# Two product columns and half an output block moved ahead of a score block, in a gated linear attention with a bilinear feed-forward on one core

## The chip, the cores and the metric

The kernel runs on one core of a Trainium2 chip, as one launch. The metric is the device time of a run in microseconds; the time of a kernel is the median over its runs. The engines are named as in the profile: PE is TensorE's matrix multiplication and PEld its weight load, DVE is VectorE, ACT is ScalarE, POOL is GpSimd and SP is SyncE. PSUM is the memory that PE writes its results to; the kernel uses it as eight banks, 0 to 7. SBUF is the core's working memory.

## The reference

For 4 batches with 8 heads of 48 numbers and 768 steps, a state of 48 x 48 per head decays by `alpha`, takes in `k` times `v`, and is read by `q`. The result, 3072 tokens by 384, goes through a bilinear feed-forward of width 1536.

```python
for t in range(S):
    state = alpha[:, :, t, :, None] * state + np.einsum('bhd,bhe->bhde', k[:, :, t], v[:, :, t])
    y[:, :, t] = np.einsum('bhd,bhde->bhe', q[:, :, t], state)
...
x = attn_out.transpose(0, 2, 1, 3).reshape(B * S, H * D)
a = x @ w_a
b = x @ w_b
out = a * b @ w_out
```

## The kernel before

The steps are cut into six chunks, numbered 0 to 5; each holds 256 steps of two of the four batches, and its two batches are called u = 0 and u = 1. A chunk goes through two parts. The recurrence part takes logarithms of `alpha`, sums them along the steps by matrix multiplications, scales `q` and `k` with the exponentials, and computes scores between steps, masks them, multiplies them with `v`, adds what the carried state gives, and updates the state. The feed-forward part computes twelve columns `a` and twelve columns `b` of 128 numbers each, multiplies them element by element, and multiplies the products with `w_out`, in four output blocks of 128 tokens.

The order of all of this is written out by hand in a text, `PROGRAM`. Each line is `chunk: step; step; ...`, and the program is emitted exactly in that order. Every engine runs its own steps in the order of the text, one after the other, and waits at a step until what the step reads has been written and what it overwrites has been read. So a step's place in the text sets its place in the queue of each engine that it uses. A digit behind a matrix step is the PSUM bank that it writes (scores `D` and out tiles `SB` take that bank and the next).

The steps that matter here, with the line of the profile on which their instructions appear:

- `a f w i`, `b f w i` (L784): product column f for one half w of a chunk's tokens, or for all of them (`*`): three matmuls on PE into bank i. The half takes 256 columns of tokens.
- `as f w` (L790): ACT copies column `a` from PSUM to SBUF. `pr f w` (L798): DVE multiplies that copy with column `b`, which it reads from PSUM, into `prod`.
- `o m h i` (L806): half h of output block m, six matmuls on PE. The first half opens bank i, the second one (`-`) adds to it. `ot m E` (L821 on ACT, L823 on DVE) brings the block to SBUF, `st m Y` stores it from SP's queue.
- `D u h i` (L672): scores of batch u, four heads, 16 matmuls on PE. `Mc` (L681) copies them on ACT to the tile `m`, `Mm` (L685) masks that tile on DVE; `M` (L677) does both on DVE.
- `SB u i` and `SA u` (L701): 16 matmuls each, the part that the carried state gives. `Y u` (L722): 32 matmuls with the masked scores. `X u E` (L762) brings the result to SBUF, and `XT u` (L769) turns it by a DMA on SP's queue into `xT`, which the product columns read.
- `k u g E` (L660 and L661): two instructions on DVE that update the state.
- `ln` (L418): the logarithms, one long instruction on ACT. `R 0`, `R 1` (L495, tiles `lh` and `ll`): rests of the pair sums on DVE. `AQ i` (L505): the sums along the steps on PE, into banks i and i + 1. `lv` (L524): scaling of `q` or `k`, here on POOL.

The place of the change is lines 129 to 141 of the kernel. There the feed-forward of chunk 1 is worked in between the last scores of chunk 2 and the sums of chunk 3:

```
2: SB 1 3; D 0 1 1; Mc 0 1; Mm 0 1 V; k * 1 V
3: R 1
1: o 2 1 -; ot 2 S
0: st 2 Y
1: st 2 Y
2: D 0 0 5; Mc 0 0; Mm 0 0 V; SB 0 1; SA 1; Y 1; X 1 S; XT 1
1: a 4 1 7
4: ln *
1: as 4 1; b 9 1 0; pr 9 1; o 0 0 5
3: AQ 3
2: SA 0; Y 0; X 0 S; XT 0
5: ld a * Y
1: o 0 1 -; ot 0 V; a 1 1 6; a 10 1 1; as 1 1; as 10 1
```

`SB 1 3` opened banks 3 and 4 for batch 1, `SB 0 1` opens banks 1 and 2 for batch 0. `AQ 3` uses banks 3 and 4 again, and `a 10 1 1` uses bank 1 again.

Of the kernel before, what the change touches and what calls it, by code (L numbers as in the profile page):

```python
# [130 lines left out]
1: o 2 1 -; ot 2 S  # L131
0: st 2 Y
1: st 2 Y
2: D 0 0 5; Mc 0 0; Mm 0 0 V; SB 0 1; SA 1; Y 1; X 1 S; XT 1
1: a 4 1 7
4: ln *
1: as 4 1; b 9 1 0; pr 9 1; o 0 0 5
3: AQ 3
2: SA 0; Y 0; X 0 S; XT 0
5: ld a * Y  # L140
1: o 0 1 -; ot 0 V; a 1 1 6; a 10 1 1; as 1 1; as 10 1
3: E 0 b; E 0 i
1: b 4 1 2; pr 4 1; b 8 1 5; b 1 1 1; a 8 1 6; b 10 1 0; pr 1 1; o 3 0 2; pr 10 1; as 8 1; pr 8 1; o 3 1 -; ot 3 S; st 3 Y
2: a 4 * 7; as 4 *
# [818 lines left out]
```

## Time and profile before

| | |
|---|---|
| time, median of 3 runs | 194.72 us (194.59 to 195.71) |
| the profiled execution | 195.32 us, of which its span is 193.5 us |
| granted clock of TensorE over the span | 1.00 |
| ACT, DVE, POOL busy | 103.3 us, 138.4 us, 50.8 us |

The span is the stretch from the first to the last instruction that the profile shows; all places below are microseconds from its start. The timeline has one row for each run of like instructions: start, length, engine, line, operation, what it writes and reads, and behind an x how many. A note in brackets says how long the engine was idle before it and who ended that. The chain of waits goes from the end of the program back, at each step to what released it. "issue" in it is time in which the engine waited for nothing that the profile shows. Ends of matmuls are modelled, so a row of matmuls may reach into the next one.

### The profile page before, as it was taken

The numbers are of one execution on the slowest core, as the hardware profiler recorded it, in microseconds if no ns is written. First come the engines' busy times: TensorE is split into PE (matmuls) and PEld (weight loads), VectorE is DVE, ScalarE is ACT, GpSimd is POOL, SyncE is SP. The second block draws the span as 40 slices with busy tenths as digits, with TensorE's granted clock in tenths as the row PEclk, the third lists the DMA queues.
The fourth block names the chain that finished last, engine by engine and source line by source line (L and its number), as shares of the span: only waits on it lengthen the run. The fifth ranks groups of instructions, "written<-read, shape, count | busy, mean of one in ns | idle before, by whom it ended". The sixth has DMA issues, their size and how long they took to land.

```text
span 193.5 us, 5877 instructions
## 1 busy us (share of the span) xinstructions
PE 184.7 (95%) x2509; PEld 111.4 (58%) x2509; DVE 138.4 (71%) x230; ACT 103.3 (53%) x189; POOL 50.8 (26%) x71
## 2 busy tenths in 40 slices
PE   7889699999999998999999999999999999999993
PEld 3467475666687865744556644555544566544462
DVE  4688777999899799597979499875854871156520
ACT  4565575886775676556565235875255622154401
POOL 8999645850640425000400020050000000000000
PEclk9999999999999999999999999999999999999999
DMA  5999999999999999489995488999297005021013
GB/s 139 261 214 211 243 247 251 252 246 260 243 220 231 198 234 219 57 233 213 172 219 69 100 203 178 118 191 120 59 180 160 3 3 122 0 99 67 0 42 122
DMA packets 67162, 30.96 MB, mean 160 GB/s; under 512 B 58064, under 2 KB 65120, under 8 KB 67136
## 3 DMA queue, kind: packets, MB, share of 16 engines
q0 software_dynamic: 18640, 14.16, 41.3%
q1 hardware_dynamic: 48352, 16.34, 39.9%
q8 instruction: 19, 0.31, 0.7%
q10 hardware_dynamic: 144, 0.10, 0.2%
q14 instruction: 7, 0.06, 0.1%
HBM read 25.98 MB, written 4.74 MB: 159 GB/s over the span
## 4 chain that ended last, share of the span: by engine, by line
PE 84%; POOL 6%; DMA 5%; issue 2%; DVE 1%; ACT 0%; POOLq 0%; DVEq 0%
PE psum L784 47%; PE psum L806 24%; DMA wb_t<-in_moe_w_b_dram 5%; PE psum L672 3%; PE psum L722 2%; PE psum L625 2%; PE psum L696 2%; PE psum L701 1%; PE psum L505 1%; PE psum L817 1%; POOL v_t L411 1%; POOL a_t L411 1%; PE psum L591 1%; POOL wa_t L391 1%; DVE prod L798 1%
## 5 line engine op out<-in xcount | busy, mean ns | idle before, releaser
L784 PE MATMUL psum<-xT,wb_t 128*128 128x512 bf16 (+1 forms) x270 | 57.0, 337 | 1.3 <-DMA wb_t<-in_moe_w_b_dram 1.3
L784 PE MATMUL psum<-xT,wa_t 128*128 128x512 bf16 (+1 forms) x270 | 56.1, 337 | 0.0
L806 PE MATMUL psum<-wo_t,prod 128*128 128x384 bf16 x276 | 48.5, 326 | 0.0
L784 PEld LDWEIGHTS <-wb_t 128*128 128x128 bf16 x270 | 25.5, 98 | 21.9 <-DMA wb_t<-in_moe_w_b_dram 1.6
L784 PEld LDWEIGHTS <-wa_t 128*128 128x128 bf16 x270 | 25.6, 98 | 19.7 <-issue 0.2
L806 PEld LDWEIGHTS <-prod 128*128 128x128 bf16 x276 | 26.1, 98 | 17.0
L681 ACT ACTIVATE m<-psum 128x1024 bf16<-128x1024 f32 x16 | 16.3, 1023 | 6.1 <-PE psum L672 5.9
L823 DVE COPY ot<-psum 128x384 f32<-128x384 f32 (+1 forms) x13 | 6.9, 538 | 15.7 <-PE psum L806 13.2
L524 POOL TENSOR_TENSOR q_t<-q_t,ra 128x384 f32<-128x384 f32 x8 | 8.8, 1103 | 34.7 <-DVE prod L798 18.4
L821 ACT ACTIVATE ot<-psum 128x384 f32<-128x384 f32 (+1 forms) x12 | 5.7, 477 | 12.9 <-PE psum L806 11.9
L524 POOL TENSOR_TENSOR k_t<-k_t,a_t 128x384 f32<-128x384 f32 x5 | 6.0, 1197 | 22.8 <-DVE QKp L550 17.9
L685 DVE TENSOR_TENSOR m<-m,mask 128x1024 bf16<-128x1024 bf16 x16 | 11.6, 734 | 0.3 <-ACT m L681 0.2
L418 ACT ACTIVATE la<-a_t 128x1536 f32<-128x1536 f32 (+2 forms) x9 | 9.5, 1053 | 3.7 <-DMA a_t<-in_alpha_dram 3.7
L550 DVE TENSOR_TENSOR QKp<-k_t,invb 128x768 bf16<-128x768 f32 x10 | 11.0, 1105 | 0.2
L677 DVE TENSOR_TENSOR m<-psum,mask 128x1024 bf16<-128x1024 f32 x8 | 9.8, 1219 | 1.6 <-PE psum L672 1.5
L550 DVE TENSOR_TENSOR QKp<-q_t,beta 128x768 bf16<-128x768 f32 x10 | 9.3, 947 | 0.0
L672 PE MATMUL psum<-kqT 64*64 64x128 bf16 x384 | 8.6, 218 | 0.2 <-DVE kqT L599 0.2
L411 POOL DMA_DIRECT2D v_t<-in_v_dram x8 | 8.6, 1075 | 0.6 <-PE psum L784 0.5
L762 ACT ACTIVATE ys<-psum 128x768 bf16<-128x768 f32 x7 | 5.6, 808 | 5.6 <-PE psum L722 3.3
L672 PEld LDWEIGHTS <-kqT 64*64 64x64 bf16 x384 | 6.3, 107 | 2.7 <-issue 2.3
L411 POOL DMA_DIRECT2D a_t<-in_alpha_dram x6 | 6.3, 1043 | 5.6 <-DVE prod L798 2.9
L444 PE MATMUL psum<-wz 128*128 128x512 bf16 x17 | 5.5, 473 | 1.2 <-DVE og L336 1.2
(272 smaller groups left out, 272.0 us busy)
## 6 DMA issues: line engine op xcount, KB each, us to landing
out_dram<-ot SPq DMA_DIRECT2D x23, 192.0 KB, 2.6
a_t<-in_alpha_dram POOLq DMA_DIRECT2D x3, 768.0 KB, 14.2
k_t<-in_k_dram SPq DMA_DIRECT2D x3, 768.0 KB, 6.7
q_t<-in_q_dram POOLq DMA_DIRECT2D x2, 768.0 KB, 12.8
v_t<-in_v_dram POOLq DMA_DIRECT2D x4, 384.0 KB, 9.2
q_t<-in_q_dram SPq DMA_DIRECT2D x2, 768.0 KB, 6.7
a_t<-in_alpha_dram POOLq DMA_DIRECT2D x3, 384.0 KB, 5.7
q_t<-in_q_dram POOLq DMA_DIRECT2D x3, 384.0 KB, 13.1
```

The costliest lines, as they stand in the source:

```text
L411: eng.dma_start(out=t[:, us, hs].rearrange("p b h r d -> p (b h) (r d)"), in_=src[ch.b0 + us.start:ch.b0 + us.stop, hs, ch.s * 2 * C:(ch.s ...
L418: nc.scalar.activation(out=ch.la[:, us, hs].rearrange("p b h r d -> p (b h r d)"), in_=ch.a[:, us, hs].rearrange("p b h r d -> p (b h r d) ...
L524: eng.tensor_mul(x, x, by)
L550: eng.tensor_mul(QKp[ch.c % 2][:, u, j, :, hs, :D], src[:, u, hs].rearrange("p h r d -> p r h d"), f)
L672: nc.tensor.matmul(s2[g * HC:(g + 1) * HC, r, p, rk, :], lhsT=ch.kqT[u][rs, 1, rk, 2 * h + p, g * HC:(g + 1) * HC], rhs=queriesT(ch, u, 2 ...
L677: nc.vector.tensor_mul(m.rearrange("p r a k s -> p (r a) (k s)"), ch.s2[u, h].rearrange("p r a k s -> p (r a) (k s)"), maskn(4))
L681: nc.scalar.activation(out=m.rearrange("p r a k s -> p (r a) (k s)"), in_=ch.s2[u, h].rearrange("p r a k s -> p (r a) (k s)"), func=AF.Copy)
L685: eng.tensor_mul(x, x, maskn(4))
L784: nc.tensor.matmul(p, lhsT=(wa_t, wb_t)[w][:, kk, f * 128:(f + 1) * 128], rhs=ch.xT[:, us.start // 2:us.stop // 2, kk].rearrange("p u g s ...
L806: nc.tensor.matmul(op, lhsT=ch.prod[:, f, at:at + C], rhs=wo_t[:, f, :], start=(f == 0), stop=(f == NFF - 1))
L821: nc.scalar.activation(out=o_, in_=i_, func=AF.Copy)
L823: eng.tensor_copy(o_, i_)
```

## The change

The product columns `a 4 1` and `b 9 1`, the copy and the multiplication that belong to them (`as 4 1`, `pr 9 1`), and the first half of output block 0 go ahead of the scores `D 0 0` of chunk 2. Their banks become 5, 6 and 7 in place of 7, 0 and 5. The second half of output block 0, with its copy to SBUF, goes from behind `Y 0` to behind `Y 1`. No step is added or taken away.

```diff
@@ -131,14 +131,14 @@
 1: o 2 1 -; ot 2 S
 0: st 2 Y
 1: st 2 Y
+1: a 4 1 5; as 4 1; b 9 1 6; pr 9 1; o 0 0 7
 2: D 0 0 5; Mc 0 0; Mm 0 0 V; SB 0 1; SA 1; Y 1; X 1 S; XT 1
-1: a 4 1 7
+1: o 0 1 -; ot 0 V
 4: ln *
-1: as 4 1; b 9 1 0; pr 9 1; o 0 0 5
 3: AQ 3
 2: SA 0; Y 0; X 0 S; XT 0
 5: ld a * Y
-1: o 0 1 -; ot 0 V; a 1 1 6; a 10 1 1; as 1 1; as 10 1
+1: a 1 1 6; a 10 1 1; as 1 1; as 10 1
 3: E 0 b; E 0 i
```

## The prediction

> **What bounds the kernel now.** I read the page first, then the chain of waits around the change, then the timeline of each engine there.
>
> ```profile
> span 193.5 us, 5877 instructions
> PE 184.7 (95%) x2509; PEld 111.4 (58%) x2509; DVE 138.4 (71%) x230; ACT 103.3 (53%) x189; POOL 50.8 (26%) x71
> ...
> q8 instruction: 19, 0.31, 0.7%
> ```
>
> PE is busy for 95% of the span, so a time moves only where PE's idle time moves: the change adds and drops no instruction. The chain of waits from 70 us on shows where PE's idle time lies here (start, length, what):
>
> ```profile
> 70.69 1.08 PE psum L806 x6
> 71.77 0.35 PE psum L672 x16
> 72.11 0.12 PE psum L701 x16
> 72.23 1.26 issue
> 73.50 0.31 PE psum L701 x16
> 73.81 0.51 PE psum L722 x32
> 74.32 0.76 PE psum L784 x6
> 75.08 0.97 PE psum L806 x6
> 76.05 0.63 PE psum L505 x8
> 76.69 0.12 PE psum L701 x14
> 76.80 0.51 PE psum L722 x32
> ```
>
> Matched with the program of order: 70.69 is `o 2 1`, 71.77 the scores `D 0 0 5`, 72.11 `SB 0 1`, 73.50 `SA 1`, 73.81 `Y 1`, 74.32 `a 4 1 7` and `b 9 1 0`, 75.08 `o 0 0 5`, 76.05 `AQ 3`, 76.69 `SA 0`, 76.80 `Y 0`; `o 0 1`, `a 1 1` and `a 10 1` follow. There is one hole, 1.26 us ahead of `SA 1`, and the profile finds nothing that `SA 1` waited for. Behind it the chain is PE work piece by piece, with no second hole. So the change can gain 1.26 us at most here, and any new wait of PE costs its full length.
>
> What is the hole? Within 70.5 to 71.6 us the queue list shows one packet of the queue of kind "instruction" (packets, MB, share):
>
> ```profile
> q8 instruction: 1, 0.02, 6.6%
> ```
>
> Nineteen such packets carry 0.31 MB, 16 KB each, and PE has 2509 + 2509 instructions, about 19 times 256. I read the hole as PE's next instructions arriving late. That packet was under way before 71.70, where the first moved matmul will start, so the change shouldn't shift its arrival: the hole ends near 73.50 whatever PE does meanwhile. The Trainium skill ("Runtime: NRT & Kernel Launch", section "Instruction fetch mechanics") says that instructions are refilled in blocks of 16 KiB, 256 instructions, and that crossing a block is mostly hidden. The size agrees with the row; "hidden" would make the hole something else, which is a rival below.
>
> **The change part by part.** It moves `a 4 1`, `b 9 1` and `o 0 0` (12 matmuls) ahead of `D 0 0`, and `o 0 1` to just behind `Y 1`; with them `as 4 1` (ACT) goes ahead of `Mc 0 0`, `pr 9 1` (DVE) ahead of `Mm 0 0`, and `ot 0` (DVE) to behind `Mm 0 0` as before. It issues no DMA and changes nothing on POOL. On SP no entry passes another. The new banks are 5 and 6 for the two products. `D 0 0 5` writes banks 5 and 6, so it must now wait until `as 4 1` and `pr 9 1` have read them; before, both products used banks (7 and 0) that `D 0 0` doesn't touch. `pr 9 1` stands in DVE's queue behind everything written above it, `R 1` (L495, `ll`) last. DVE's timeline of before:
>
> ```profile
> 70.01 0.95 DVE L495 TENSOR_TENSOR lh<-l 128x768 f32<-128x768 f32 x1
> ...
> 71.79 0.69 DVE L685 TENSOR_TENSOR m<-m,mask 128x1024 bf16<-128x1024 bf16 x1 [0.24 <-ACT m L681]
> 72.40 0.55 DVE L660 TENSOR_TENSOR tmp<-psum,Sm 128x384 f32<-128x384 f32 x1
> 72.99 0.56 DVE L661 TENSOR_TENSOR S<-tmp,bl 128x384 bf16<-128x384 f32 x1
> 73.46 1.76 DVE L495 TENSOR_TENSOR ll<-lh 128x768 f32<-128x768 f32 x1
> 75.14 1.49 DVE L685 TENSOR_TENSOR m<-m,mask 128x1024 bf16<-128x1024 bf16 x1
> 76.56 0.44 DVE L798 TENSOR_TENSOR prod<-as__1484,psum 128x256 bf16<-128x256 bf16 x1
> ```
>
> DVE is full from 71.79 (`Mm 0 1`) over `k * 1` to the end of `R 1`. `Mm 0 0` starts at 75.14; that place is now `pr 9 1`'s, which ends at 75.14 + 0.44 = 75.58. Nothing ahead of it on DVE is touched, so this is when `D 0 0` may start. The starts on PE, for step lengths:
>
> ```profile
> 71.70 0.42 PE L672 MATMUL psum<-kqT 64*64 64x128 bf16 x16
> 73.74 0.57 PE L722 MATMUL psum<-v_t,m 64*128 64x48 bf16 x32
> 74.25 0.50 PE L784 MATMUL psum<-xT,wa_t 128*128 128x256 bf16 x3
> 74.59 0.49 PE L784 MATMUL psum<-xT,wb_t 128*128 128x256 bf16 x3
> 75.98 0.36 PE L505 MATMUL psum<-l,utb 64*64 64x384 bf16 x4
> 76.74 0.57 PE L722 MATMUL psum<-v_t,m 64*128 64x48 bf16 x32
> 77.24 1.15 PE L806 MATMUL psum<-wo_t,prod 128*128 128x384 bf16 x6
> 78.23 0.82 PE L784 MATMUL psum<-xT,wa_t 128*128 128x256 bf16 x6
> ```
>
> From start to start one product takes 0.33 (74.25 to 74.59), half an output block 0.99 (77.24 to 78.23), `Y` 0.5 (73.74 to 74.25, 76.74 to 77.24), `AQ` with `SA` 0.76 (75.98 to 76.74). The 78.23 row holds `a 1 1` and `a 10 1`. New PE order: `a 4 1` at 71.70, `b 9 1` 72.03, `o 0 0` 72.37, ready for `D 0 0` at 73.36. It starts at 75.6. First new wait: 2.2 us. With `D`, `SB`, `SA` at 0.35 + 0.12 + 0.12 = 0.59 from the chain (the 0.31 of the `SA` behind the hole is a restart), `Y 1` starts at 76.2, `o 0 1` at 76.7, and PE is ready for `AQ` at 77.7.
>
> Now ACT, whose rows are:
>
> ```profile
> 71.80 0.49 ACT L821 ACTIVATE ot<-psum 128x384 f32<-128x384 f32 x1
> 72.19 1.02 ACT L681 ACTIVATE m<-psum 128x1024 bf16<-128x1024 f32 x1
> 74.36 0.81 ACT L762 ACTIVATE ys<-psum 128x768 bf16<-128x768 f32 x1 [1.15 <-PE psum L722]
> 75.07 1.48 ACT L418 ACTIVATE la<-a_t 128x1536 f32<-128x1536 f32 x1
> ```
>
> `o 0 0 7` writes the bank that `ot 2` reads until 71.80 + 0.49 = 72.29: just free at 72.37, so nothing. `as 4 1` runs at once behind it, before 72.7: nothing. `Mc 0 0` (the 1.02 row) starts when `D 0 0` is through, 75.6 + 0.42 = 76.0, and ends at 77.1; `X 1` (0.81) follows at once and ends at 77.9. `AQ 3` writes the banks that `X 1` reads: it starts at 77.9, a second wait of 0.2, where 1.6 us of products and `o 0 0` used to cover `X 1`. Then `Y 0` at 78.66; its second half needs `Mm 0 0`, which DVE, idle since 75.58, does at 77.1 to 77.8 in its 0.69 of the 71.79 row: covered. `a 1 1` starts at 79.16. But `ln *` (1.48) stands between `X 1` and `X 0` on ACT. Before, it ran from 75.07 under PE's products; now it runs from 77.9 to 79.3, so `X 0` runs 79.3 to 80.1. `a 10 1 1` writes bank 1, which `X 0` reads, and `o 0 1`, which used to stand there for 0.99 us, is gone: `a 10` starts at 80.15, a third wait of about 0.65. Before, `a 10` started one product into the row of 78.23, at 78.56.
>
> Sum: 2.2 + 0.2 + 0.65 = 3.05 of new idle time, less the hole's 1.26 and its restart's 0.2: **+1.6 us**, the same as 80.15 - 78.56. Behind it the order is unchanged and PE works without a break, so nothing gives it back. The tightest neighbour is `XT 0`, a transpose by DMA which SP starts when `X 0` is through and whose result `a 4 *` needs:
>
> ```profile
> DMA to landing us min/median/max: 3.1/3.1/3.1
> 82.50 0.81 PE L784 MATMUL psum<-xT,wa_t 128*128 128x512 bf16 x3
> ```
>
> It would start at 80.15 and land at 83.3; PE comes at 82.50 + 1.6 = 84.1. Covered, with 0.8 to spare.
>
> Bounds. What I know least is `R 1`: the same operation took 0.95 at 70.01 and 1.76 at 73.46, where POOL was at work:
>
> ```profile
> 73.24 2.84 POOL L524 TENSOR_TENSOR k_t<-k_t,a_t 128x384 f32<-128x384 f32 x2 [4.47 <-DMA k_t<-in_k_dram]
> ```
>
> I take 1.76, since neither POOL's start (a DMA's landing) nor `R 1`'s moves; at 0.95 all of the sum from 75.6 on is 0.8 earlier, +0.8. `pr 9 1` could be stretched in the same way, by up to the 0.8 that `R 1` and `Mm 0 0` (1.49 against 0.69) show; it reads PSUM, so I take 0.44. The Trainium skill ("SBUF — State Buffer", section "SBUF: two separate sides") says that GpSimd and a VectorE operation with two SBUF inputs exclude each other for a whole instruction; the rows agree for `R 1`, and by it `pr 9 1` with one SBUF input is spared. Lastly, PE's next 256 instructions: their packet would be asked for up to 2 us later than before, so a second late arrival of up to about 0.4 beside the third wait is possible; I take 0.
>
> The profiled execution took 195.32, 1.8 over its span and 0.6 over the median, so its 196.9 becomes **194.72 + 1.6 = 196.3** for the median.
>
> **The rivals.** *The hole isn't there to be absorbed* (chance 0.18): the profiled execution is 0.6 slower than the median, and if ordinary ones have little or none of the hole, or it has another cause and stays ahead of `SA 1`, the new waits cost up to 1.6 + 1.26 = 2.9, 197.6. For it: the skill's "mostly hidden", and 195.71 as the highest of three runs; against it: the packet's place. *A free `R 1`* (0.13): if `k_t` lands only after `R 1` has begun, or much earlier, POOL and `R 1` don't meet, and it ends at 74.4: +0.8, 195.5. *The moved work fills the hole and costs nothing* (0.09): 12 matmuls of 1.66 us cover 1.26, `D 0 0` follows at once, 194.72 - 1.26 = 193.5. It decides on `pr 9 1`: it must start before about 73.0, ahead of `R 1`. DVE's rows speak against it, `k * 1` and `R 1` standing back to back from 72.40 to 75.2.
>
> **How the numbers follow.** The forecast has 0.60, with its own range 195.9 to 196.9 (0.4 less, 0.6 more). From 195.3 to 197.7 lie it, the free `R 1` and most of the first rival. One per cent, about what a measurement of this kernel can tell from no change, is 1.95 us: slower means above 196.67. Of the forecast some 0.17 lies there, with the first rival's 0.18: 0.35. Faster by over 1% needs more than the hole: 0.03 of the third rival. The rest, 0.62, is within 1%, on the slow side.
>
> **What would show it.** In the changed profile: the hole ahead of `SA 1` gone; `D 0 0` (L672) starting at about 75.6, 2.2 us after the end of `o 0 0`, released by DVE L798, with `ll` at 73.46 just ahead of that L798; L505 released by ACT L762; `la` (L418) at about 77.9 and an L784 at about 80.1 released by ACT L762. The prediction is wrong if L672 starts before 74.5, if a hole for no reason stays at `SA 1`, or if PE makes up time behind 80 us.

## The result, and the profile after

| | before | changed |
|---|---|---|
| median of 19 runs each | 195.06 us | 196.34 us |
| lowest and highest | 194.19, 196.05 | 195.51, 199.09 |
| profiled execution, span | 195.32, 193.5 | 196.22, 194.4 |

The ratio of the changed kernel to the one before is 1.0076, with a 95% interval of 1.0049 to 1.0102: slower by 1.5 us, where +1.6 was forecast; the two medians differ by 1.3 us. The ratios in this document are formed over the runs, not from the two medians, and leave out each run that lies over 1.5% above the fastest of its kernel, here the four from 198.49 to 199.09; with them the mean is 1.9 us over that of before. Ten of the changed kernel's 19 runs lie between 195.51 and 196.34, the other nine between 197.16 and 199.09; the runs of the kernel before have no such second group.

PE's waits between 66 and 86 us in the profile after (who waited for whom: us in total, times, longest), and PE's timeline from 72 us on, of which the small matmuls of L701 are left out:

```profile
PE psum L672 <- DVE prod L798: 1.2, 1, 1.2
PE psum L784 <- ACT ys L762: 0.5, 1, 0.5
```

```profile
72.48 1.14 PE L806 MATMUL psum<-wo_t,prod 128*128 128x384 bf16 x6
73.54 0.24 PE L672 MATMUL psum<-kqT 64*64 64x128 bf16 x1
74.95 0.41 PE L672 MATMUL psum<-kqT 64*64 64x128 bf16 x15 [1.17 <-DVE prod L798]
75.55 0.57 PE L722 MATMUL psum<-v_t,m 64*128 64x48 bf16 x32
76.05 1.15 PE L806 MATMUL psum<-wo_t,prod 128*128 128x384 bf16 x6
77.19 0.36 PE L505 MATMUL psum<-l,utb 64*64 64x384 bf16 x4
...
78.44 0.50 PE L784 MATMUL psum<-xT,wa_t 128*128 128x256 bf16 x3
79.42 0.49 PE L784 MATMUL psum<-xT,wa_t 128*128 128x256 bf16 x3 [0.47 <-ACT ys L762]
```

The hole ahead of `SA 1` is gone, and two new waits stand in its place. `D 0 0` issues one matmul, into bank 5, at 73.54, and then waits at the second, into bank 6, until `pr 9 1` (L798) has read it. `a 10 1` waits for `X 0` (L762). The releasers on DVE, ACT and POOL:

```profile
73.60 0.95 DVE L495 TENSOR_TENSOR ll<-lh 128x768 f32<-128x768 f32 x1
74.47 0.43 DVE L798 TENSOR_TENSOR prod<-as__1484,psum 128x256 bf16<-128x256 bf16 x1
```

```profile
75.41 1.02 ACT L681 ACTIVATE m<-psum 128x1024 bf16<-128x1024 f32 x1 [2.71 <-PE psum L672]
76.33 0.80 ACT L762 ACTIVATE ys<-psum 128x768 bf16<-128x768 f32 x1
77.02 1.49 ACT L418 ACTIVATE la<-a_t 128x1536 f32<-128x1536 f32 x1
78.55 0.81 ACT L762 ACTIVATE ys<-psum 128x768 bf16<-128x768 f32 x1
```

```profile
73.85 2.52 POOL L524 TENSOR_TENSOR k_t<-k_t,a_t 128x384 f32<-128x384 f32 x2 [4.93 <-DMA k_t<-in_k_dram]
```

`pr 9 1` stands directly behind `R 1`, as forecast, but `R 1` took 0.95 here, not 1.76: POOL began at 73.85, after `R 1` at 73.60; in the profile of before POOL was first (73.24 against 73.46). So this execution shows the smaller of the two losses. By starts, `a 10` runs at 79.42; PE ran 0.13 later already at `o 2 1` (70.75 against 70.62 in the PE timelines), so the stretch lost 79.42 - 78.56 - 0.13 = 0.73.

### The profile page after: what moved, and what is told of

Read it like the earlier page. It is cut to its first block, busy times and chain, and to the rows that moved or that the text cites. A ratio compares the mean times of both kernels' runs of the same rounds, so it can differ in the third digit from the quotient of the medians.

```text
span 194.4 us, 5876 instructions
## 1 busy us (share of the span) xinstructions
PE 186.0 (96%) x2509; PEld 112.6 (58%) x2509; DVE 136.3 (70%) x230; ACT 103.3 (53%) x189; POOL 50.6 (26%) x71
## 4 chain that ended last, share of the span: by engine, by line
PE 83%; POOL 6%; DMA 5%; DVE 2%; issue 1%; ACT 1%; POOLq 0%
PE psum L784 47%; PE psum L806 23%; DMA wb_t<-in_moe_w_b_dram 5%; PE psum L672 3%; PE psum L722 2%; PE psum L625 2%; PE psum L696 2%; PE psum L701 1%; PE psum L505 1%; PE psum L817 1%; POOL v_t L411 1%; POOL a_t L411 1%; DVE prod L798 1%; PE psum L591 1%; POOL wa_t L391 1%
## 5 line engine op out<-in xcount | busy, mean ns | idle before, releaser
L685 DVE TENSOR_TENSOR m<-m,mask 128x1024 bf16<-128x1024 bf16 x16 | 10.8, 686 | 1.8 <-ACT m L681 1.8
L672 PE MATMUL psum<-kqT 64*64 64x128 bf16 x384 | 8.8, 218 | 1.5 <-DVE prod L798 1.4
L672 PEld LDWEIGHTS <-kqT 64*64 64x64 bf16 x384 | 6.4, 107 | 4.2 <-issue 3.8
L762 ACT ACTIVATE ys<-psum 128x768 bf16<-128x768 f32 x7 | 5.5, 807 | 4.0 <-PE psum L701 2.3
```

The lines of the kernel that those rows point to most:

```text
L672: nc.tensor.matmul(s2[g * HC:(g + 1) * HC, r, p, rk, :], lhsT=ch.kqT[u][rs, 1, rk, 2 * h + p, g * HC:(g + 1) * HC], rhs=queriesT(ch, u, 2 ...
L685: eng.tensor_mul(x, x, maskn(4))
```

## The experiments

Each is timed in its own session against the kernel before, whose median there was 195.2 to 195.4; so ratios are compared, not times. Where a kernel has a line less (the first part alone, and those with early stores), the line numbers of its profile are one lower: L671 there is L672 here.

**The bank of `b 9 1`.** In the changed kernel, so that `D 0 0` no longer meets `pr 9 1`:

```diff
-1: a 4 1 5; as 4 1; b 9 1 6; pr 9 1; o 0 0 7
+1: a 4 1 5; as 4 1; o 0 0 7; b 9 1 0; pr 9 1
```

> The changed kernel with one difference: b 9 1 goes to bank 0, as before the change, and stands behind o 0 0 (bank 0 is free by then), so that the scores D 0 0 no longer wait for pr 9 1. Theory (most of the loss is D 0 0 waiting for pr 9 1): D 0 0 (L672) starts at about 73.8 with no wait for DVE, a 10 1 at 78.3 to 78.6, as in the kernel before (78.56); time 194.6 to 195.2, ratio to before 0.998 to 1.001. Rival (the loss comes from a 10 1 waiting for X 0, whose cover o 0 1 is gone, and from X 0's place on ACT): the wait for X 0 stays at 0.5 or more and the time at 195.8 or above, ratio 1.004 or more.

Measured: 195.73, ratio 1.0021 (0.9986 to 1.0056): most of the loss is gone. `D 0 0` starts at 73.60 and doesn't wait (`o 0 0` ahead of it waits 0.25 for `ot 2`). But nothing is gained either, and the chain of waits shows why:

```profile
73.67 0.35 PE psum L672 x16
74.02 0.25 PE psum L701 x32
74.27 0.51 PE psum L722 x32
...
77.18 0.33 PE psum L784 x2
77.50 1.92 issue
79.42 2.26 PE psum L784 x19
```

PE gets through `SA 1` without a hole and is ready for the third matmul of `a 1 1` at 77.5; there it waits 1.92 us for nothing that the profile shows. From `SA 1`'s first matmul to that one the kernel before has 16 + 32 + 3 + 3 + 6 + 12 + 16 + 32 + 6 + 2 = 128 matmuls, with a weight load each: 256 instructions, one instruction packet. What PE won at the one packet it lost at the next. Nor did `a 10` have to wait for `X 0`, which ended under the new hole. The place of the loss was as the theory had it. The time was not: 195.73 lies over its 194.6 to 195.2, and `a 10` comes behind 79.4 in place of 78.3 to 78.6.

**`pr 9 1` ahead of `R 1`.** In the changed kernel, DVE's order alone:

```diff
-3: R 1
 1: o 2 1 -; ot 2 S
...
 1: a 4 1 5; as 4 1; b 9 1 6; pr 9 1; o 0 0 7
+3: R 1
```

> The changed kernel with R 1 (chunk 3) moved behind pr 9 1 in the text; only DVE's order changes, the banks stay. Theory (pr 9 1 is late because it is queued behind R 1, 0.95 to 1.76 us): pr 9 1 starts at about 73.6 and D 0 0 at about 74.0 in place of 74.9 to 75.6; a 10 1 at about 78.5; time 194.7 to 195.3, and the spread of the runs smaller than the changed kernel's (195.5 to 199.1), because R 1's meeting with POOL no longer reaches PE. Rival (D 0 0 waits for something else, such as as 4 1 on ACT): D 0 0 stays at 74.9 or later and the time at 196.3.

Measured: 195.45, ratio 1.0000 (0.9971 to 1.0030). Of its 12 runs, eleven lie between 194.63 and 196.24; the twelfth, the profiled one, took 374.52 and isn't read. So this rests on the times alone: the expected start of `D 0 0` is seen in no trace of this kernel, but with the same order and the early stores, below, the wait is 0.3. The interval lies wholly under the changed kernel's. With the banks as changed, the place behind `R 1` in DVE's queue is what costs.

**Is the hole a late instruction packet?** In the kernel before, 12 small matmuls of zeros early on, where PE waits anyway:

```diff
-0: b 0 0 4; a 0 0 2; as 0 0; pr 0 0
+0: warm 12 4; b 0 0 4; a 0 0 2; as 0 0; pr 0 0
```

> The kernel before with 12 small matmuls of zeros (128 x 128) ahead of b 0 0 of chunk 0, where PE waits for a weight load anyway; everything behind them stands 24 PE instructions later in the instruction stream. Theory (the 1.26 us hole ahead of SA 1 is the next 256 PE instructions arriving late): the hole moves 12 matmuls earlier, to behind the 4th matmul of SB 0 1, with the same order of length, and the 17th to 20th wait nowhere. Rival (SA 1 waits for data or for a resource of its own): the hole stays ahead of SA 1, behind 16 matmuls of SB 0 1.

Measured: one execution, 197.24, which is not compared. In it the hole is not at the packet that begins in `SB 0 1` but at the following one, 128 matmuls on. PE's timeline of `Y 0`, which in the kernel before is one row of 32:

```profile
76.13 0.37 PE L722 MATMUL psum<-v_t,m 64*128 64x48 bf16 x16
77.12 0.32 PE L722 MATMUL psum<-v_t,m 64*128 64x48 bf16 x12 [0.63 <-DVE m L685]
78.85 0.22 PE L722 MATMUL psum<-v_t,m 64*128 64x48 bf16 x4 [1.41 <-issue]
```

The hole stands behind the 28th matmul of `Y 0`. The third of `a 1 1` less 12 is exactly that: two of `a 1 1`, six of `o 0 1`, four of `Y 0`. The step expected within `SB 0 1` was off by one packet; the rival, a need of `SA 1`'s own, is out. The packets' own times in the traces say the same: in each of the seven profiles of these experiments and of before that have such a hole, PE goes on 1.3 to 1.65 us after a packet of the instruction queue has ended (71.86 and 73.50 in the kernel before, 77.99 and 79.42 in `x_bank`, 77.41 and 78.85 here). A hole that is always at the same instruction number, whatever the instruction there does, whose neighbours wait for nothing, and that ends at about the same distance behind such a packet, is an instruction packet that comes late.

**The second part alone.** In the kernel before, `o 0 1` and `ot 0` go from behind `Y 0` to behind `o 0 0`.

> The kernel before with the second part of the change alone: o 0 1 and ot 0 go from behind Y 0 to behind o 0 0, ahead of AQ 3; the banks and everything else stay. Theory (o 0 1 was the cover of X 0): AQ 3 and Y 0 come 1.0 us later, a 10 1 waits 0.4 to 0.6 us for X 0 behind a 1 1, and the time is 0.4 to 0.6 over the kernel before, 195.4 to 195.7. Rival (X 0 is covered anyway): no wait, the time of before.

Measured: 195.69, ratio 1.0009 (0.9978 to 1.0040), too near to tell. Its chain of waits:

```profile
72.03 0.25 PE psum L701 x32
...
77.08 0.45 issue
```

The second row is a hole at the third matmul of `a 1 1`, right ahead of where `X 0` would be waited for. The first is `SB 0 1` and `SA 1` without a hole, though PE's program up to there is that of the kernel before: the packet began at 68.98 in this execution, not at 70.70. So the hole ahead of `SA 1` comes and goes with the packet's time. The experiment was repeated with the early stores below.

**POOL held back behind `R 1`.** In the changed kernel, a one-element copy on POOL that reads `R 1`'s tile goes ahead of the two scalings of `k`:

```diff
-3: ra 1; lv 1 q P; ld v * P; lv 0 k P; lv 1 k P
+3: ra 1; lv 1 q P; ld v * P
...
-3: R 1
+3: R 1; gater; lv 0 k P; lv 1 k P
```

> The changed kernel, with POOL's two scalings of k for chunk 3 held back until R 1 has written its tile (a one-element copy on POOL that reads R 1's tile stands ahead of them), so that POOL and R 1 never meet. Theory (R 1 takes 0.95 alone and up to 1.76 beside POOL, and D 0 0 waits for it through pr 9 1): R 1 0.95 in the profile, D 0 0 0.9 to 1.2 us behind o 0 0, time 195.9 to 196.2, at the low end of the changed kernel's runs (195.5 to 199.1) and without the runs above 197. Rival (the long runs of the changed kernel have another cause): the same spread as the changed kernel's, with nearly half of the runs above 197.

Measured: 196.18 (195.50 to 196.86), ratio 1.0047 (1.0026 to 1.0067). All ten runs lie under 197. DVE's timeline in its profile has `R 1` and `pr 9 1`:

```profile
73.83 0.95 DVE L495 TENSOR_TENSOR ll<-lh 128x768 f32<-128x768 f32 x1
74.70 0.43 DVE L798 TENSOR_TENSOR prod<-as__1482,psum 128x256 bf16<-128x256 bf16 x1
```

So the changed kernel's upper group of runs goes back to the meeting of POOL and `R 1`. The changed kernel itself was not run in that session; but with the early stores, below, its POOL begins at 74.52, when `R 1` is through, and none of its seven runs is over 196.55. The same edit of the kernel before:

> The kernel before with POOL's scalings of k for chunk 3 held back behind R 1, as was done to the changed kernel. Theory (in the kernel before no matmul waits for R 1 or for pr 9 1 in this stretch, so R 1's length does not reach PE): the time of before within 0.3, its spread unchanged. Rival (R 1's meeting with POOL costs the kernel before as well): faster by 0.4 or more.

Measured: 195.16, ratio 0.9994 (0.9966 to 1.0021): nothing. Before the change no matmul hung on `R 1` here; the change is what tied PE to it. That holds where the hole stands: in `b_shift`, without a hole at `SA 1` and with an `R 1` of 1.75, `Y 0` waits 0.63 for `Mm 0 0` behind it.

**A meeting made on purpose.** As above, and POOL's `lv 1 q` is put beside `k * 1`.

> The same, but POOL's scaling of q for batch 1 of chunk 3, which was done at 66 us, is put where DVE does k * 1 and R 1 (released by Mm 0 1); the scalings of k stay held back behind R 1. Theory: DVE is held up by POOL by 0.5 to 0.9 us ahead of pr 9 1, D 0 0 starts that much later than in x_gate, and the time is 0.5 to 0.9 over x_gate's, 196.6 to 197.0, or more where PE's longer idle time costs clock. Rival (DVE's delay doesn't reach PE): the time of x_gate.

Measured: 200.12, ratio 1.0151 (1.0088 to 1.0215), and no test of the theory. Without `lv 1 q` ahead of it, POOL's load of `v` was issued at 63.51 in place of 67.72, and the scores ahead of this stretch waited 4.3 us for their transpose by DMA; that the one brought the other is likely and not shown. `k * 1`'s second instruction did take 1.12 in place of 0.56 beside POOL. The case came about by itself in the next kernel.

**The first part alone.** In the changed kernel, `o 0 1` and `ot 0` go back behind `Y 0`.

> The first part of the change alone: the changed kernel with o 0 1 and ot 0 put back behind Y 0. Theory: D 0 0 waits for pr 9 1 as in the changed kernel (1.2 us, or 2 where R 1 meets POOL); AQ 3 then waits 0.9 to 1.1 us for X 1, which has lost the products that stood between; a 10 1 waits for nothing; 0.2 to 0.5 over the changed kernel, 196.5 to 196.9. Rival (moving o 0 1 is what costs): under 196.0.

Measured: 198.75, ratio 1.0139 (1.0090 to 1.0187), far over the 0.2 to 0.5 that were expected. PE's waits in its profile, the rows of DVE and POOL in the timeline, the chain, and the busy times by stretch (length, busy time and instructions of PE, PEld, DVE, ACT and POOL, granted clock, DMA share, GB/s):

```profile
PE psum L671 <- DVE prod L797: 2.0, 1, 2.0
PE psum L504 <- ACT ys L761: 1.1, 1, 1.1
```

```profile
73.54 1.75 DVE L494 TENSOR_TENSOR ll<-lh 128x768 f32<-128x768 f32 x1
```

```profile
73.49 2.66 POOL L523 TENSOR_TENSOR k_t<-k_t,a_t 128x384 f32<-128x384 f32 x2 [4.64 <-DMA k_t<-in_k_dram]
```

```profile
78.82 0.23 PE psum L700 x11
79.06 0.75 PE psum L721 x32
79.81 2.01 PE psum L805 x6
```

```profile
75.00:78.00 3.00, 1.23 (x83) 1.19 (x86) 1.34 (x3) 1.84 (x3) 1.15 (x1) 1.00 0.29 64
78.00:81.00 3.00, 3.00 (x65) 2.08 (x64) 0.00 (x0) 2.06 (x2) 0.00 (x0) 0.54 0.37 71
81.00:84.00 3.00, 3.00 (x25) 2.38 (x23) 1.40 (x3) 1.61 (x5) 0.00 (x0) 0.89 0.42 80
```

Both waits are as expected, the first in its long form: `R 1` met POOL and took 1.75. What was not expected stands behind them. The granted clock is 0.54 and 0.89 of full speed in two stretches of 3 us, so PE lost (0.46 + 0.11) x 3 = 1.7 us, and the six matmuls of `o 0 1` took 2.01, where the kernel before has 1.08. The Trainium skill ("TensorE: Matmul & The Clock Gate", section "Part 1: The HAM clock gate (the "warmup" mystery)") gives half rate after an idle window of about 3.4 us; here it fell after waits of 2.0 and 1.1 us with work between them; the measurement decides.

**Calmer transfers when the packet is asked for.** In the kernel before, two stores go into SP's queue where their blocks are ready:

```diff
-0: st 3 Y; o 1 1 -; ot 1 V
+0: st 3 Y; o 1 1 -; ot 1 V; st 0 Y; st 1 Y
...
-0: st 0 Y; o 2 1 -
+0: o 2 1 -
...
-0: st 1 Y
```

> The kernel before with the stores of output blocks 0 and 1 of chunk 0 put into SP's queue 9 us earlier, at 57 to 59 us behind the store of block 3, where they were ready; in the kernel before they go out from 67 us on, when PE's instruction packet is asked for. Theory (the packet is held up by other transfers): the packet starts earlier than 3.1 us behind the start of PE's block, the holes in PE at 72 to 79 us become shorter by 0.3 to 1.2 us in sum, and the time is 0.2 to 0.8 less than before, 194.3 to 195.1. Rival (the packet takes its 5 to 6 us whatever else moves): the time of before.

Measured: 194.81, ratio 0.9974 (0.9952 to 0.9996), faster than either kernel, if only just clear of the kernel before. The chain of waits in its profile:

```profile
72.31 0.35 PE psum L671 x16
72.66 0.25 PE psum L700 x32
72.91 0.51 PE psum L721 x32
...
77.71 0.14 issue
```

`SB 0 1` and `SA 1` are one piece of 32; of the hole 0.14 is left, at the next packet. `b_second` shows that one profile without the hole proves little. The packets' times say more: in the four profiles with early stores the packet of this place begins between 69.2 and 70.0; of the eight without (`x_cont`, which runs late, and the 374.52 execution of `x_prfirst` left out), seven have it between 70.19 and 70.99, and `b_second` at 68.98. The edit also does something else: SP issues the load of `k` at 68.00 in place of 66.40, and POOL's scaling begins at 75.25, when `R 1` is through. How much of the 0.26% is the packet's and how much this is open.

**Early stores with the changed order**, with `R 1` behind `pr 9 1` and without.

> The changed kernel with R 1 behind pr 9 1 and with the early stores together. Theory: the waits for pr 9 1 are short and the instruction packets come earlier, so it stands no worse than the early stores alone, 194.2 to 195.1; what is left is a 10 1's wait for X 0 or for the instructions. Rival: PE is held by the instruction packets alone, and the order of the products adds nothing: equal to the early stores within 0.2.

> The changed kernel with the early stores of blocks 0 and 1 of chunk 0, its banks and DVE's order untouched. Theory (the changed kernel's own waits already cover the late instructions, so shortening those brings it nothing): D 0 0 waits 1.1 to 1.2 us for pr 9 1, a 10 1 waits 0.4 to 0.6 for X 0, time 196.0 to 196.4, that is 1.2 to 1.6 over the kernel before with the same early stores (194.81). Rival (the early stores help whatever order follows): 0.5 under the changed kernel's 196.34, 195.8 or less.

Measured: 195.57, ratio 1.0008 (0.9989 to 1.0027), and 196.28, ratio 1.0060 (1.0037 to 1.0083). PE's waits in the two, in this order:

```profile
PE psum L783 <- ACT ys L761: 0.5, 1, 0.5
PE psum L671 <- DVE prod L797: 0.3, 1, 0.3
```

```profile
PE psum L671 <- DVE prod L797: 1.2, 1, 1.2
PE psum L783 <- ACT ys L761: 0.5, 1, 0.5
```

Against the early stores alone, by the ratios and with 195.3 for the kernel before, the changed order costs what its waits are: (1.0060 - 0.9974) x 195.3 = 1.7 for 1.2 + 0.5, and (1.0008 - 0.9974) x 195.3 = 0.7 for 0.3 + 0.5. The first of the two runs (`x_stores`) was expected to lose nothing against the early stores alone, and that was wrong. The stores gave the changed kernel itself little to nothing (1.0060 against 1.0076); that its own waits already lay over the late packets fits its profile.

**The second part alone, with early stores.**

> The kernel before with the early stores and with the second part of the change alone (o 0 1 and ot 0 ahead of AQ 3), now that the late instructions hide less. Theory: a 10 1 waits 0.3 to 0.5 us for X 0, and the time is 0.3 to 0.5 over the kernel before with early stores (194.81): 195.1 to 195.3. Rival: no wait, 194.8.

Measured: 194.68, ratio 0.9975 (0.9954 to 0.9997), the time of the early stores alone, where 195.1 to 195.3 was expected. `X 0` ended at 77.48 + 0.81 = 78.29, but a hole of 0.90 for instructions held `a 1 1` until 78.67, so the wait for `X 0` lay under it. Alone, that part costs nothing that shows.

## Why the prediction was right

- *Nothing is gained by filling the hole.* Right, and for more than the stated reason. `x_bank` takes away the wait for `pr 9 1`, fills the hole with 12 matmuls and gains nothing, since in its profile a hole of 1.92 stands at the next packet. The third rival (193.5) was not to be had by this order.
- *The hole is a late instruction packet, and the change doesn't shift its arrival.* The first half is shown by `b_shift` and by the packets' times. In the profile after, the packet ended at 72.21, 0.35 later than before, and `D 0 0`'s wait until 74.95 lies over it. That the hole ends near 73.50 whatever happens is too strong: in `b_second` the packet came 1.7 earlier and there was no hole. How often an ordinary execution has the hole no run shows directly; the times of the short runs, below, speak against the first rival.
- *`D 0 0` waits for `pr 9 1`, which waits behind `R 1`.* Shown by the releasers in the profile after, by `x_prfirst`, where DVE's order alone is undone (ratio 1.0000 against 1.0076), and by `x_bank` (1.0021, whose interval still touches the changed kernel's). One sign of being wrong, L672 starting before 74.5, did come: the first matmul of `D 0 0`, into bank 5, ran at 73.54. The prediction took `D 0 0` as one piece; the other 15 waited as it said.
- *Its size.* Forecast 2.2 us; by starts it is 74.95 - (72.48 + 0.99) = 1.5 in the profile after and 75.70 - (72.42 + 0.99) = 2.3 in `x_first`'s. The term that was mis-sized is `R 1`: 0.95 or 1.75, by whether POOL's scaling or `R 1` begins first. I took one value for both, "since neither POOL's start (a DMA's landing) nor `R 1`'s moves"; POOL's start moves from one profiled execution to the next (73.24 before, 73.85 after, 73.49 in `x_first`). The second rival, a free `R 1`, with 0.13, is what the profiled execution shows and, by their times, ten of 19 runs.
- *`pr 9 1` is not stretched.* Right: 0.43 beside POOL.
- *`AQ` waits for `X 1` by 0.2, `a 10` for `X 0` by 0.65.* By starts 0.15 (77.19 against 76.05 + 0.99; the profile does not list it as a wait, but `X 1` ended at 77.13) and 0.65 (79.42 against 78.44 + 0.33). `ln *` adds nothing where `R 1` is free: it ended at 78.5, when `Y 0` did.
- *The sum.* +1.6 came out as +1.3 by the medians and +1.5 by the ratio, from two cases neither of which is +1.6. Ten runs lie around 196.1, about +1: with `R 1` free, the new waits are 1.5 + 0.15 + 0.65 = 2.3, and less the hole's 1.26 and the restart's 0.2 that makes +0.8; were the hole missing from most executions of the kernel before, it would be +2.3. The other nine are at +2 to +4. `x_gate`, and `a_stores` beside it, show that they go back to `R 1`'s meeting with POOL. The granted clock of the runs, which is on record, shows much of the rest: it is 0.983 to 0.991 in seven of the nine and in one of the ten, and 0.009 of a span of 194 is 1.7 us, the loss that `x_first`'s profile shows in its two stretches. The two that kept their clock took 197.16 and 197.47, +2.1 and +2.4, still over the +1.6 of this case. That the clock's fall is what lengthens the seven is likely and not shown: no profile of the changed kernel fell there, and three runs of the kernel before with 0.99 took only 194.4 to 194.7.
- *The time.* 196.3 was forecast and the median is 196.34, and that close a hit is luck. The 194.72 that it started from, a median of three runs, was 0.3 under that of 19, the step between the medians is 0.3 short of 1.6, and the median is the longest of the ten short runs.
- *PE makes nothing up behind 80 us.* Right: behind the stretch PE stays late by the same amount to the end in the profile after.

## What to carry to other kernels

When a step is moved ahead of another, look at every engine that it uses: a matmul that shares a PSUM bank with a moved product inherits the whole queue that stands ahead of that product's reader. A hole in PE that waits for nothing, and that stays at the same instruction number when work is moved across it, may only move on to the next packet when it is filled with work; look at the packets of the instruction queue and at what else moves in the DMA queues then. And where a step's length depends on which of two engines comes first, forecast two times, not one.

## What the runs showed of the hardware

- PE's instructions come 256 at a time: 19 packets of 16 KB for 5018 matmuls and weight loads, and holes that stand 128 matmuls with their weight loads apart (`before`, `x_bank`). Where small matmuls use up such a packet in 3.6 to 5.1 us, the next one can be late: by 1.26 in the kernel before, 0.45 in `b_second`, 1.92 in `x_bank`. PE goes on 1.3 to 1.65 us behind the packet's end. The Trainium skill ("Runtime: NRT & Kernel Launch", section "Instruction fetch mechanics") calls the crossing of a block mostly hidden; in this stretch it was not. The edit that takes two stores of 192 KB out of the packet's way, and delays the load of `k` with it, gained 0.26%.
- `R 1` took 0.95 when it began before POOL's scaling and 1.75 when POOL was first (73.49 against 73.54 in `x_first`); the one that was first kept its length, `R 1` 0.95 after the change and POOL's first scaling 0.98 in `x_first`. The Trainium skill ("SBUF — State Buffer", section "SBUF: two separate sides") has this as an exclusive lock that goes to whoever starts first, and the rows agree.
- PE's granted clock can fall to about a half for a few us, 0.54 over 78 to 81 us, after waits of 2.0 and 1.1 us (`x_first`).
